# Windowed attention and a spatially gated MLP on one core: a written-out order of 1113 steps is replaced by another

## The chip, the core and the metric

The kernel runs on one core of a Trainium2 chip. The core has five engines with a queue each, which run their own instructions in order and wait for one another through semaphores: TensorE (PE), VectorE (DVE), ScalarE (ACT), GpSimd (POOL) and SyncE (SP), which here issues the transfers. The metric is the device time of one execution in microseconds, and what is compared is the median of several executions.

## What is computed

Eight batches of eight heads, 576 positions and 64 values per head go through causal attention with a window of 64. The result, 512 values per position, goes through a gated MLP whose gate is mixed over positions.

```python
# q, k, v: (8, 8, 576, 64) float32
scores = q @ k.transpose(0, 1, 3, 2) / sqrt(64)
attn = softmax(where((rel >= 0) & (rel < 64), scores, -1e9))      # rel = row - column
x = heads_side_by_side(attn @ v)                                  # (8, 576, 512)
h = maximum(x @ w_in, 0.0)                                        # w_in: (512, 1024)
u, v = h[..., :512], h[..., 512:]
v_n = (v - mean(v)) / sqrt(var(v) + 1e-6)
v_s = einsum('ts,bsd->btd', w_spatial, v_n) + b_spatial[None, :, None]
out = (u * v_s) @ w_out                                           # (8, 576, 512)
```

## The kernel before

The kernel builds a list of steps, each with a name, a function that issues its instructions and the buffers that it takes. A long string, ORDER, names all 1113 steps in the order in which they are issued; each word is `step:engine:buffer`. The engines' queues run side by side, so the string sets the order on each engine, the engine of each step that can run on several, and the buffer or PSUM bank that it gets. There is no other scheduling.

The steps of batch b (0 to 7); g is a half of four heads, u a pair of heads in it:

- `ldq`, `ldk`, `ldv`: loads, on SP (lines 424 and 445). `cq`, `ck`: casts of q and k to 16 bits; `tq`, `tk`: transposes of them on DVE (line 431). `cv`, `sl`, `su`, `s4`: v cast and copied once more, shifted by 64 positions. These casts and copies (helper `cp`, lines 316 to 324) can run on ACT or POOL, in the first two batches on DVE too. On POOL a cast of q or k is three instructions.
- `S`: scores, 56 small matmuls into a pair of banks (line 491); `E`: exp on ACT (498); `M`: the mask, as a minimum, on DVE (501); `Z`: sums of the exps by matmul (514); `N`, `n`: ln and exp on ACT, which give the inverse (541, 543); `P`: the product with v (526); `X`: the product of both on DVE (534). The last 64 positions of all heads have steps of their own, with `r` in their names.
- `V`: the gate half of x times w_in (four row blocks, and `V_4` for the last 64 rows, which also computes the last rows of the output of the batch before); `Vr`: relu on ACT (660); `Vb`, `Va`: mean and variance on DVE (662, 664); `L1`, `L2`: the inverse root on ACT (707, 709); `A`: the normalization on DVE (719).
- `U`: the other half, `Ur`: its relu on ACT (748); `G`: the mixing over positions; `Ge`: the gating on DVE (778); `O`: the product with w_out; `Oe`: its copy out of PSUM on ACT (637); `st`: stores, on SP.

A G needs all five A of its batch, an O the Ge of rows 0 to 3, a V all four X; every PE step also needs the bank that it writes to be emptied by the step that reads it. The four single banks and two pairs of banks are handed out in ORDER. Casts of the weights are `cwin`, `cwsp`, `cwo`, `cb`; `W` transposes w_spatial and `We` copies it out. `D` are 27 matmuls of zeros that fill PE early on.

The wide matmuls of V, U, G and O run through `halves`. A step in the set HALVED issues each matmul as two with 64 columns of weights (line 613), which keeps the array divided as Z and P have it; any other issues one with 128 (line 610). Before, the set comes from a rule on the neighbours in ORDER and holds 92 steps.

Of the kernel before, what the change touches and what calls it, by code (L numbers as in the profile page):

```python
# [24 lines left out]
M0_11:DVE ldv0_04:DQ Z0_00:PE:1 E0_r0:ACT:0 sl0_10:DVE:0 cv0_00:DVE:1 E0_r1:ACT Z0_10:PE:2
ldv0_13:DQ M0_r:DVE Z0_01:PE:3 ldv0_14:DQ N0_10:ACT:0 D10:PE:0 sl0_00:DVE:1 N0_01:ACT:1 su0_00:DVE
ldwin110:DQ:7 cv0_01:DVE N0_00:ACT:2 ldwin111:DQ su0_01:DVE sl0_01:POOL Z0_r:PE:2 su0_10:DVE
Z0_11:PE:3 ldwin101:DQ N0_r:ACT:3 D9:PE:0 s40_0:POOL tk1_0:DVE:5 n0_00:ACT ldb:DQ:1 D8:PE:1
ldk1_1:DQ:2 n0_10:ACT D13:PE:2 ldq1_1:DQ:3 n0_01:ACT P0_01:PE:0 cv0_11:DVE ldwin000:DQ:0 P0_00:PE:1
sl0_11:DVE su0_11:POOL N0_11:ACT:4 S1_0:PE:0:1 ldwin001:DQ X0_00:DVE:0 ldwin010:DQ:4 n0_11:ACT  # L30
cwin110:POOL D20:PE:2 s40_1:DVE ldwin011:DQ E1_00:ACT:1 D19:PE:3 cwin111:POOL X0_01:DVE P0_10:PE:1
ldwsp3:DQ:5 P0_11:PE:2 cwin101:POOL E1_01:ACT:0 X0_10:DVE:1 D18:PE:3 ldwsp2:DQ:7 D3:PE:0 X0_11:DVE
cwin100:ACT P0_r:PE:1 M1_00:DVE n0_r:ACT cb:ACT V0_1:PE:3 ldwsp1:DQ:6 M1_01:DVE ck1_1:POOL:2
V0_2:PE:0 X0_r:DVE:0 Vr0_1:ACT:0 ldwsp4:DQ:1 Z1_00:PE:2 Vb0_1:DVE:0 V0_0:PE:1 N1_00:ACT:5
ldv1_00:DQ:2 cq1_1:POOL:3 tk1_1:DVE:0 Vr0_2:ACT:1 V0_3:PE:3 Vr0_0:ACT:2 cwin000:ACT ldwsp0:DQ:2
n1_00:ACT Z1_01:PE:2 V0_4:PE:0 D25:PE:1 D26:PE:1 ldv1_01:DQ cwin010:POOL tq1_1:DVE:1 cwin001:ACT
N1_01:ACT:2 cwin011:POOL ldv1_02:DQ Vr0_3:ACT:3 Vb0_2:DVE:1 S1_1:PE:0:1 cwsp3:POOL ldv1_03:DQ
Vr0_4:ACT:4 Vb0_0:DVE:2 U0_2:PE:1 E1_11:ACT:2 cwsp2:POOL Vb0_3:DVE:3 U0_3:PE:2 Va0_2:DVE cwsp1:POOL
E1_10:ACT:3 Va0_3:DVE Va0_1:DVE Vb0_4:DVE:4 U0_4:PE:3 Va0_0:DVE Va0_4:DVE M1_11:DVE ldv1_04:DQ
L10:ACT:0 U0_1:PE:0 Ur0_3:ACT:0 M1_10:DVE ldk2_0:DQ:3 Ur0_2:ACT:1 S1_r:PE:1:0 ldv1_10:DQ:3 cwsp4:DVE  # L40
Z1_11:PE:2 L20:ACT Ur0_1:ACT:2 U0_0:PE:1 A0_4:DVE cwsp0:DVE E1_r0:ACT:1 ldv1_11:DQ E1_r1:ACT
A0_0:DVE:0 Ur0_4:ACT:3 W0:PE:0 A0_3:DVE:1 ldq2_0:DQ:0 N1_11:ACT:1 cv1_00:DVE:2 cv1_01:POOL W2:PE:3
ldv1_12:DQ M1_r:DVE Ur0_0:ACT:4 W3:PE:2 ldv1_13:DQ sl1_00:ACT:2 sl1_01:POOL W4:PE:1 We0:DVE
s41_0:ACT We2:DVE We3:ACT W1:PE:0 su1_01:POOL su1_00:DVE Z1_r:PE:3 We4:ACT ldv1_14:DQ ck2_0:POOL:0
A0_2:DVE:2 P1_01:PE:2 N1_r:ACT:0 P1_00:PE:1 ldk2_1:DQ:4 Z1_10:PE:3 A0_1:DVE:3 ldwo10:DQ:5 We1:DVE
N1_10:ACT:4 ldq2_1:DQ:7 X1_00:DVE:2 G0_4:PE:0 n1_01:ACT ldwo00:DQ:6 G0_3:PE:3 n1_10:ACT ldwo11:DQ
cv1_10:POOL:3 X1_01:DVE ldwo01:DQ tk2_0:DVE:2 sl1_10:ACT:3 su1_10:POOL G0_0:PE:1 cq2_0:ACT:1
ldq3_0:DQ:1 cv1_11:POOL ldv2_00:DQ:0 Ge0_3:DVE:0 s41_1:POOL G0_2:PE:2 sl1_11:ACT Ge0_4:DVE:1
su1_11:POOL n1_r:ACT tq2_0:DVE:3 n1_11:ACT ldk3_0:DQ:2 G0_1:PE:3 ck2_1:POOL:2 cwo10:ACT ldv2_01:DQ
Ge0_2:DVE:2 P1_10:PE:0 P1_11:PE:2 X1_10:DVE:3 S2_0:PE:1:0 X1_11:DVE cq2_1:POOL:3 ldv2_02:DQ  # L50
P1_r:PE:0 E2_00:ACT:0 Ge0_0:DVE:3 U1_2:PE:2 ldv2_03:DQ Ge0_1:DVE:4 E2_01:ACT:1 U1_1:PE:1 X1_r:DVE:1
M2_00:DVE Ur1_2:ACT:5 V1_3:PE:3 cwo01:POOL tk2_1:DVE:0 cwo11:ACT Ur1_1:ACT:0 cwo00:POOL V1_1:PE:0
Vr1_3:ACT:5 M2_01:DVE cq3_0:POOL:0 V1_2:PE:2 Vr1_1:ACT:6 ldv2_10:DQ:1 Vb1_3:DVE:5 V1_4:PE:1
ldv2_11:DQ tq2_1:DVE:1 Vr1_2:ACT:7 Z2_01:PE:3 Vr1_4:ACT:4 V1_0:PE:0 ck3_0:POOL:1 Vb1_2:DVE:1
N2_01:ACT:3 tq3_0:DVE:4 S2_1:PE:1:0 Oe0_4:ACT:0 ldv2_12:DQ Vr1_0:ACT:2 U1_0:PE:2 ldk3_1:DQ:3
cv2_00:POOL:1 Va1_2:DVE E2_11:ACT:3 Va1_3:DVE ldv2_13:DQ Vb1_1:DVE:3 Z2_00:PE:3 O0_2:PE:1 ldv2_14:DQ
Vb1_0:DVE:0 E2_10:ACT:2 Vb1_4:DVE:2 ldv2_04:DQ U1_4:PE:0 N2_00:ACT:5 Va1_1:DVE ldv3_10:DQ:2
S2_r:PE:0:1 Va1_0:DVE Va1_4:DVE tk3_0:DVE:5 L11:ACT:1 O0_0:PE:3 Oe0_2:ACT:0 ldq3_1:DQ:0 E2_r0:ACT:0
ldv3_11:DQ Ur1_4:ACT:3 M2_11:DVE U1_3:PE:1 L21:ACT ldv3_12:DQ E2_r1:ACT A1_4:DVE Oe0_0:ACT:1
O0_1:PE:0 A1_2:DVE:4 ldq4_0:DQ:4 Ur1_0:ACT:1 A1_3:DVE:5 ldv3_13:DQ A1_1:DVE:6 Ur1_3:ACT:4  # L60
S3_0:PE:0:1 A1_0:DVE:7 ldv5_10:DQ:3 n2_00:ACT M2_10:DVE Z2_11:PE:3 Oe0_1:ACT G1_0:PE:2 M2_r:DVE
sl2_00:ACT:0 su2_00:POOL Z2_r:PE:1 N2_11:ACT:2 G1_3:PE:0 Ge1_0:DVE:5 s42_0:ACT cv2_10:POOL:0
N2_r:ACT:4 ldv3_00:DQ:0 n2_01:ACT Z2_10:PE:3 Ge1_3:DVE:6 P2_00:PE:2 ldq4_1:DQ:7 N2_10:ACT:1
O0_3:PE:1 ldk4_0:DQ:5 X2_00:DVE:0 sl2_10:ACT:1 su2_10:POOL P2_01:PE:0 G1_4:PE:3 s42_1:ACT X2_01:DVE
n2_10:ACT ck3_1:POOL:2 P2_10:PE:2 Ge1_4:DVE:7 n2_11:ACT P2_11:PE:0 X2_10:DVE:1 G1_1:PE:3 E3_01:ACT:0
X2_11:DVE cq3_1:POOL:3 n2_r:ACT V2_3:PE:2 Ge1_1:DVE:8 E3_00:ACT:1 M3_01:DVE V2_2:PE:0 Oe0_3:ACT
M3_00:DVE U2_2:PE:3 st0_1:DQ Vr2_2:ACT:3 tk3_1:DVE:0 ldv4_00:DQ:1 Vr2_3:ACT:1 U2_0:PE:1 cq4_0:POOL:0
ldv3_01:DQ Ur2_2:ACT:2 tq3_1:DVE:1 Z3_00:PE:0 ldv3_02:DQ V2_0:PE:2 N3_00:ACT:0 ldv3_03:DQ
cq4_1:POOL:1 Vb2_3:DVE:4 Ur2_0:ACT:1 S3_1:PE:1:0 n3_00:ACT tq4_0:DVE:2 P2_r:PE:3 U2_3:PE:0
E3_11:ACT:2 cv3_10:POOL:2 ldv3_14:DQ X2_r:DVE:0 E3_10:ACT:3 V2_1:PE:1 Vb2_2:DVE:1 st0_4:DQ  # L70
tq4_1:DVE:3 ck4_0:POOL:2 ldk4_1:DQ:6 U2_4:PE:3 Vr2_0:ACT:0 st0_0:DQ S3_r:PE:0:1 Vr2_1:ACT:4
V2_4:PE:2 ldv3_04:DQ M3_10:DVE Ur2_4:ACT:4 Ur2_3:ACT:3 sl3_10:POOL:2 Z3_01:PE:1 E3_r0:ACT:1
# [796 lines left out]
```

## Time and profile before

| | |
|---|---|
| median of three runs | 199.47 us (199.40 to 200.56) |
| the profiled execution | 199.64 us, of which the span of instructions is 197.9 us |
| clock granted to TensorE, mean | 0.996 |
| moved by DMA | 42.71 MB, 216 GB/s over the span |

A profile page lists the busy time of each engine and its share of the span, then the span in 40 slices of 4.95 us, one digit for each: the busy tenths. PEld is the loading of weights, which overlaps the matmuls. A row of a group gives line, engine, operation, output and input tiles, shapes and count, then the time that the group keeps the engine busy, the mean of one in ns, and the idle time before them with what ended it. A row of the timeline gives start and length in us, engine, line, operation, tiles, shapes and count; in square brackets is idle time before it. The chain of waits follows the last instruction back, at each step to what released it: start, length, what.

### The profile page before, as it was taken

What the parts mean: (1) busy time and instruction counts of PE and PEld (TensorE: products, weight loads), DVE (VectorE), ACT (ScalarE), POOL (GpSimd) and SP (SyncE); (2) the same over time, 40 slices, a digit from 0 to 9 for tenths busy, and PEclk for the clock granted to TensorE, in tenths of its full rate; (3) what the DMA queues carried; (4) which work ended last, traced back from release to release, by engine and by line L of the source; (5) the groups of instructions that cost most, each with busy time, mean ns of one, the idle gap of its engine ahead of it and who ended that gap; (6) DMA issues with size and microseconds to landing.
All of it is one profiled execution on the core that took longest, in us unless ns stands there. A gap on an engine that the chain in (4) does not pass through costs nothing.

```text
span 197.9 us, 7455 instructions
## 1 busy us (share of the span) xinstructions
PE 186.3 (94%) x3145; PEld 108.1 (55%) x3145; DVE 158.2 (80%) x306; ACT 169.0 (85%) x305; POOL 77.8 (39%) x147
## 2 busy tenths in 40 slices
PE   7688999997999999999999999999999999999991
PEld 2333556664556755575476566466465565754450
...
ACT  2589889887899999999999999999999999558341
POOL 5232863964858797212999199100000000000000
...
GB/s 224 389 289 200 392 358 249 292 374 360 133 235 313 274 213 280 314 196 285 282 259 250 278 261 49 251 202 229 238 107 65 47 45 2 215 0 3 181 110 187
DMA packets 50276, 42.71 MB, mean 216 GB/s; under 512 B 39361, under 2 KB 39489, under 8 KB 50242
## 3 DMA queue, kind: packets, MB, share of 16 engines
...
## 4 chain that ended last, share of the span: by engine, by line
ACT 40%; PE 27%; DVE 17%; DMA 6%; SPq 4%; issue 4%; ACTq 0%; DVEq 0%
PE bank L613 14%; PE bank L610 8%; ACT e L498 7%; ACT ob L637 5%; ACT ru L748 5%; ACT lz L541 5%; ACT hs L316 4%; ACT lz L543 4%; SPq L445 4%; DMA nv<-in_v_dram 3%; ACT vs L660 3%; DMA nk<-in_k_dram 2%; DVE kT L431 2%; DVE e L501 2%; DVE qT L431 2%
## 5 line engine op out<-in xcount | busy, mean ns | idle before, releaser
L498 ACT ACTIVATE e<-pair 128x1024 f16<-128x1024 f32 x32 | 31.9, 1025 | 2.8 <-PE pair L491 2.6
L613 PE MATMUL bank<-wspT,vn 128*64 128x512 f16 (+3 forms) x440 | 32.4, 296 | 0.3
L778 DVE TENSOR_TENSOR g<-bank,ru 128x512 f16<-128x512 f32 (+1 forms) x40 | 24.6, 630 | 9.4 <-PE bank L610 4.4
L662 DVE BATCH_NORM_STATS2 st<-vs 128x6 f32<-128x512 f16 (+1 forms) x40 | 26.0, 672 | 3.5 <-ACT vs L660 3.4
L660 ACT ACTIVATE vs<-bank 128x512 f16<-128x512 f32 (+1 forms) x40 | 23.3, 601 | 5.7 <-PE bank L613 3.9
L534 DVE TENSOR_TENSOR x<-bank,lz 128x512 f16<-128x512 f32 x32 | 21.4, 683 | 5.7 <-PE bank L526 3.9
L748 ACT ACTIVATE ru<-bank 128x512 f32<-128x512 f32 (+1 forms) x40 | 21.7, 564 | 5.0 <-PE bank L610 4.4
L637 ACT COPY ob<-bank 128x512 f32<-128x512 f32 (+1 forms) x39 | 22.9, 592 | 2.1 <-PE bank L610 1.9
L613 PEld LDWEIGHTS <-vn 128*64 128x64 f16 (+1 forms) x440 | 18.7, 110 | 10.8 <-issue 1.2
L501 DVE TENSOR_TENSOR e<-e,mask 128x1024 f16<-128x1024 f16 x32 | 22.1, 706 | 1.2 <-ACT e L498 1.2
L319 POOL CAST hk<-nk 128x384 f16<-128x384 f32 x33 | 16.4, 531 | 16.1 <-DMA nk<-in_k_dram 15.3
L613 PE MATMUL bank<-x,win 128*64 128x512 f16 (+1 forms) x288 | 22.3, 298 | 0.0
L613 PE MATMUL bank<-win,x 128*64 128x512 f16 x184 | 22.1, 379 | 0.2 <-DVE x L603 0.2
L431 DVE STREAM_TRANSPOSE qT<-hq 128x576 f32<-128x576 f32 x16 | 19.8, 1238 | 2.3 <-POOL hq L319 2.3
L431 DVE STREAM_TRANSPOSE kT<-hk 128x576 f32<-128x576 f32 x16 | 19.9, 1244 | 0.2 <-ACT hk L316 0.2
L543 ACT ACTIVATE lz<-lz 128x512 f32<-128x512 f32 x32 | 19.8, 637 | 0.1
L541 ACT ACTIVATE lz<-bank 128x512 f32<-128x512 f32 x32 | 18.6, 607 | 1.2 <-PE bank L514 1.0
L719 DVE TENSOR_SCALAR vn<-vs,mv,ln 128x512 f16<-128x512 f16 (+1 forms) x40 | 15.6, 442 | 4.8 <-ACT ln L709 4.7
L319 POOL CAST hq<-nq 128x384 f16<-128x384 f32 x30 | 15.3, 545 | 8.3 <-DMA nq<-in_q_dram 5.7
L322 POOL COPY hs<-hv 64x512 f16<-64x512 f16 (+1 forms) x28 | 15.6, 588 | 5.0 <-issue 4.3
L818 PE MATMUL bank<-scratch 128*128 128x512 f16 (+1 forms) x68 | 15.1, 372 | 1.3 <-DVE scratch L257 1.3
L613 PE MATMUL bank<-wout,g 128*64 128x512 f16 x128 | 16.1, 380 | 0.0
...
## 6 DMA issues: line engine op xcount, KB each, us to landing
nq<-in_q_dram SPq DMA_DIRECT2D x16, 576.0 KB, 6.3
nk<-in_k_dram SPq DMA_DIRECT2D x16, 576.0 KB, 5.7
...
```

The lines of the kernel that those rows point to most:

```text
L319: nc.gpsimd.tensor_copy(o[:, n:n + 384], i[:, n:n + 384])
L431: d = add(f"t{name}{b}_{g}", ("DVE", 1.09), key, lambda e: nc.vector.transpose(qt.t[:, :].rearrange("p (i j) -> p j i", j=18), h.t[:, :].b ...
L498: ex = add(f"E{b}_{g}{u}", ("ACT", 0.91), key, lambda e, u=u: nc.scalar.activation(e2[u].t[:, :, :], sc[u].t[:, :, :], AF.Exp, bias=0.0, s ...
L501: mins.append(add(f"M{b}_{g}{u}", ("DVE", 0.65), key, lambda e, u=u: nc.vector.tensor_tensor(e2[u].t[:, :, :], e2[u].t[:, :, :], mask[:, : ...
L541: a = add(f"N{tag}", ("ACT", 0.06 + 0.00083 * n), key, lambda e: nc.scalar.activation(lz.t[:, 0:n], zb.t[:, 0:n], AF.Ln), deps=[z], acq=[l ...
L543: c = add(f"n{tag}", ("ACT", 0.09 + 0.00083 * n), key, lambda e: nc.scalar.activation(lz.t[:, 0:n], lz.t[:, 0:n], AF.Exp, bias=0.0, scale= ...
L613: nc.tensor.matmul(o[c:c + 64, :], w[:, c:c + 64], x, start=start, stop=stop)
L637: lambda e: (nc.vector.tensor_copy if last else nc.scalar.copy)(view(), m.t[rows, 0:n]),
L660: rl = add(f"Vr{b}_{j}", ("ACT", 0.49), key, lambda e: nc.scalar.activation(vs.t[0:jn, :], m.t[0:jn, :], AF.Relu), deps=[pv], acq=[vs], us ...
L662: s1 = add(f"Vb{b}_{j}", ("DVE", 0.6), key + 0.02, lambda e: nc.vector.bn_stats(st6.t[0:jn, 0:6], vs.t[0:jn, :]), deps=[rl], acq=[st6], us ...
L748: lambda e, m=m, ru=ru, n=n: nc.scalar.activation(ru.t[:, 0:n], m.t[:, 0:n], AF.Relu), deps=[pu], acq=[ru], uses=[m])))
L778: lambda e, m=m, g=g, ru=ru, n=n: nc.vector.tensor_tensor(g.t[:, 0:n], m.t[:, 0:n], ru.t[:, 0:n], ALU.mult),
```

## The change

ORDER is replaced. The steps are the same, and so is the order of the 155 DMA issues of SP. New are the order of the steps on PE, ACT, DVE and POOL, the buffers and banks, the engine of 55 casts and copies, and the set of halved steps, which is now written into ORDER (engine `PH`) and holds 118: 36 that were whole are halved, 10 that were halved are whole.

```diff
 ORDER = """
-ldq0_0:DQ:0 ldk0_0:DQ:1 D14:PE:0 ldk0_1:DQ:2 ldq0_1:DQ:3 D12:PE:1 ldv0_00:DQ:0 D23:PE:2 ldq1_0:DQ:4
...
+D0:PE:0 D21:PE:1 D4:PE:2 D13:PE:3 ldq0_0:DQ:0 ldk0_0:DQ:1 D14:PE:0 D1:PE:1 cq0_0:POOL:0 tq0_0:DVE:0
...
+su1_11:POOL n1_11:ACT sl1_11:POOL P1_10:PE:2 X1_00:DVE:2 cq2_1:POOL:2 cwo00:POOL ldv2_14:DQ
...
+P1_11:PE:0 X1_11:DVE G0_0:PH:1 Ge0_0:DVE:2 ck2_1:ACT:3 ldq3_1:DQ:5 ldv3_11:DQ V1_3:PH:2 tk2_1:DVE:0
+tq2_1:DVE:1 Vr1_3:ACT:5 Vb1_3:DVE:5 sl2_00:POOL:0 V1_0:PH:0 cwo10:ACT cq3_0:POOL:1 Ge0_2:DVE:3
+Vr1_0:ACT:6 Vb1_0:DVE:1 V1_1:PH:1 Vr1_1:ACT:7 ldv3_12:DQ su2_00:POOL E2_00:ACT:1 ldq4_0:DQ:0
+ldv3_13:DQ U1_0:PH:2 V1_2:PH:0 P1_r:PE:1 Vr1_2:ACT:4 Vb1_2:DVE:2 cv2_10:POOL:0 S2_1:PE:0:1
+s42_0:POOL n1_r:ACT X1_r:DVE:1 Va1_2:DVE cwo01:DVE Ur1_0:ACT:5 E2_10:ACT:3 M2_10:DVE M2_01:DVE
+sl2_10:POOL:1 U1_2:PH:3 E2_11:ACT:2 Ur1_2:ACT:1 G0_3:PH:0 V1_4:PE:2 Oe0_4:ACT:0 Vb1_1:DVE:3
+Vr1_4:ACT:1 Va1_1:DVE s42_1:POOL cq3_1:POOL:3 U1_4:PH:1 Ur1_4:ACT:4 M2_00:DVE S2_r:PE:0:1
+E2_r0:ACT:0 E2_r1:ACT U1_3:PH:3 Ur1_3:ACT:2 Ge0_3:DVE:4 Z2_00:PE:2 N2_00:ACT:4 Va1_0:DVE O0_2:PH:1
...
-G7_0:PE:0 U7_1:PE:1 Ge7_0:DVE:5 Ge7_3:DVE:6 G7_1:PE:3 Ur7_1:ACT:1 U7_4:PE:0 Ge7_1:DVE:7 G7_4:PE:2
-Ur7_4:ACT:5 O7_2:PE:1 Ge7_4:DVE:9 O7_0:PE:3 Oe7_2:ACT:1 st7_2:DQ O7_1:PE:0 Oe7_0:ACT:0 st7_0:DQ
...
+Ur7_1:ACT:1 G7_1:PE:1 Ge7_1:DVE:6 Ge7_0:DVE:5 G7_3:PE:3 Ge7_3:DVE:7 G7_2:PE:2 G7_4:PE:1 Ge7_2:DVE:8
+O7_2:PE:0 Oe7_2:ACT:0 O7_0:PE:3 O7_1:PE:2 O7_3:PE:0 st6_1:DQ Oe7_0:ACT:1 st7_2:DQ st7_0:DQ
+Ge7_4:DVE:9 Oe7_1:ACT st7_1:DQ O7_4:PE:1 Oe7_3:ACT Oe7_4:DVE:0 st7_3:ACT st7_41:ACT st7_40:DQ
 """
...
-        out.append((by.pop(name), eng, [int(x) for x in banks]))
+        out.append((by.pop(name), "PE" if eng == "PH" else eng, [int(x) for x in banks]))
...
-def halved(longest):
...
-HALVED = halved(2) | {f"U0_{i}" for i in range(5)}
+HALVED = {w.split(":")[0] for w in ORDER.split() if w.split(":")[1] == "PH"}
```

Which casts and copies move:

| | from ACT | to ACT |
|---|---|---|
| casts of q and k | ck0_1, ck4_1, ck7_0, ck7_1, cq5_0, cq7_0, cq7_1 to POOL | ck2_1, ck3_1, ck6_1, cq5_1 from POOL |
| v: cv, sl, su, s4 | 3 cv, 8 sl, 3 su, 7 s4 to POOL | su2_10, s41_1, s45_0 from POOL |
| weights | cb, cwin001, cwo11 to POOL; cwin100, We3 to DVE | cwin111 from POOL; We0, We2 from DVE |

Between DVE and POOL: cq0_1, three cv and a sl of batch 0, cwsp0 and cwsp4 go to POOL; sl0_01, s40_0, cq1_1, su1_01 and cwo01 come from it.

More of the change, by code (lines that the diff above doesn't have):

```diff
@@ L25 @@
[L25 to L72, printed above, removed]
@@ new lines @@
+ldv2_03:DQ su1_00:DVE ck2_0:POOL:3 Z1_10:PE:0 N1_10:ACT:3 su1_01:DVE tk2_0:DVE:2 G0_4:PE:3
+Ge0_4:DVE:0 s41_0:POOL G0_1:PE:1 Ge0_1:DVE:1 cq2_0:ACT:1 sl1_01:POOL n1_00:ACT cv1_10:POOL:3
+sl1_10:ACT:3 s41_1:ACT ldv2_10:DQ:1 Z1_11:PE:2 tq2_0:DVE:3 ldv2_11:DQ N1_11:ACT:2 ldv2_12:DQ
+ldk3_1:DQ:4 ldv2_13:DQ n1_10:ACT P1_00:PE:0 G0_2:PE:3 P1_01:PE:1 S2_0:PE:1:0 su1_10:POOL cv1_11:POOL
+su1_11:POOL n1_11:ACT sl1_11:POOL P1_10:PE:2 X1_00:DVE:2 cq2_1:POOL:2 cwo00:POOL ldv2_14:DQ
+ldv2_04:DQ cwo11:POOL ck3_0:POOL:0 X1_01:DVE E2_01:ACT:0 ldv3_10:DQ:2 X1_10:DVE:3 cv2_00:POOL:1
@@ new lines @@
+A4_3:DVE:3 cq6_1:POOL:1 ldv7_02:DQ tq6_1:DVE:1 Vr5_3:ACT:1 V5_0:PH:0 Vr5_0:ACT:6 A4_4:DVE G4_3:PH:3
+M6_00:DVE S6_1:PE:1:0 E6_10:ACT:2 Ge4_3:DVE:1 Vb5_0:DVE:0 P5_r:PE:1 X5_r:DVE:1 G4_4:PH:2 Ge4_4:DVE:0
+E6_11:ACT:1 M6_01:DVE cv6_10:POOL:0 G4_1:PH:0 V5_4:PE:3 Vb5_1:DVE:5 Vr5_4:ACT:7 Z6_00:PE:1
+N6_00:ACT:0 s46_0:POOL Oe4_4:ACT:0 G4_2:PH:2 Ge4_1:DVE:2 n6_00:ACT sl6_10:POOL:1 M6_10:DVE
+Vb5_4:DVE:1 U5_2:PH:0 Ur5_2:ACT:4 Z6_10:PE:1 G4_0:PH:3 N6_10:ACT:4 n6_10:ACT Vb5_3:DVE:3 Z6_01:PE:0
+N6_01:ACT:5 Va5_4:DVE su6_00:POOL P6_00:PE:1 M6_11:DVE Ge4_2:DVE:3 s46_1:POOL Va5_0:DVE ldv7_03:DQ
@@ new lines @@
+Va6_4:DVE N7_01:ACT:2 n7_01:ACT Va6_2:DVE G5_2:PH:3 S7_r:PE:0:1 Z7_00:PE:2 N7_00:ACT:0 n7_00:ACT
+Ge5_2:DVE:8 G5_0:PH:1 Z7_10:PE:0 N7_10:ACT:4 Va6_0:DVE U6_2:PH:3 P7_01:PE:2 Ur6_2:ACT:2 P7_00:PE:0
+Ge5_0:DVE:9 O5_1:PH:1 E7_r0:ACT:1 Vb6_3:DVE:5 Va6_3:DVE O5_0:PH:3 L16:ACT:0 X7_00:DVE:2 M7_11:DVE
+L26:ACT A6_3:DVE:0 Oe5_0:ACT:1 Oe5_1:ACT X7_01:DVE O5_2:PH:0 U6_3:PH:2 Oe5_2:ACT:0 A6_0:DVE:1
+n7_10:ACT O5_3:PH:3 sl7_10:POOL:3 su7_10:POOL A6_1:DVE:2 E7_r1:ACT st5_4:DQ U6_4:PH:1 ldv7_14:DQ
+M7_r:DVE Oe5_3:ACT A6_2:DVE:3 A6_4:DVE G6_3:PH:0 Z7_11:PE:3 Ur6_4:ACT:1 s47_1:POOL Ur6_3:ACT:0
@@ L194 @@
 CHOOSE = as_listed
-def halved(longest):
-    def kind(name):
-        return "s" if name[0] == "S" else "v" if name[0] in "ZP" or (
-            name[0] == "V" and name.endswith("_4")) else "f"
-    seq = [w.split(":")[0] for w in ORDER.split() if w.split(":")[1] == "PE" and w[0] != "D"]
-    runs = []
-    for name in seq:
-        if not runs or runs[-1][0] != kind(name):
-            runs.append((kind(name), []))
-        runs[-1][1].append(name)
-    out = set()
-    for a, (what, names), c in zip([("f", [])] + runs, runs, runs[1:] + [("f", [])]):
-        near = (a[0] == "v") + (c[0] == "v")
-        if what == "f" and not any(n[0] == "W" for n in names) and (
-                near == 2 or near == 1 and len(names) <= longest):
-            out.update(names)
-    return out
-HALVED = halved(2) | {f"U0_{i}" for i in range(5)}
+HALVED = {w.split(":")[0] for w in ORDER.split() if w.split(":")[1] == "PH"}
 @with_exitstack
```

175 lines of the change are left out of this document (98 added, 77 removed).

## The prediction

> **What bounds the kernel now.** I read the page's busy shares and slices first, then a window sum, the chain of waits, and TensorE's timeline step by step.
>
> ```profile
> span 197.9 us, 7455 instructions
> PE 186.3 (94%) x3145; PEld 108.1 (55%) x3145; DVE 158.2 (80%) x306; ACT 169.0 (85%) x305; POOL 77.8 (39%) x147
> ...
> PE   7688999997999999999999999999999999999991
> ...
> ACT  2589889887899999999999999999999999558341
> POOL 5232863964858797212999199100000000000000
> ```
>
> ```profile
> 50.00:125.00 75.00, 74.40 (x1453) 44.90 (x1450) 68.39 (x124) 72.58 (x134) 51.69 (x96) 1.00 0.88 240
> ```
>
> The window's columns are length, then busy time of PE, PEld, DVE, ACT and POOL, clock, DMA share and GB/s. From the tenth slice on (about 50 us) PE is nearly always busy and ACT is busy 72.58 of 75 us; POOL has a third of its time free, and all of it after 125 us. But PE "busy" counts overlapping matmuls, so I price PE steps by the distance from one start to the next:
>
> ```profile
> 14.85 0.30 PE L559 MATMUL pair<-qT,kT 32*128 32x64 f16 x16
> 15.08 0.84 PE L514 MATMUL bank<-e,ones 128*64 128x512 f16 x6
> ...
> 21.70 0.25 PE L526 MATMUL bank<-e,hv 128*64 128x128 f16 x2
> ...
> 22.31 1.04 PE L818 MATMUL bank<-scratch 128*128 128x512 f16 x4
> ...
> 46.87 1.90 PE L613 MATMUL bank<-x,win 128*64 128x512 f16 x16
> 48.60 2.76 PE L613 MATMUL bank<-win,x 128*64 128x512 f16 x24
> 51.19 0.38 PE L693 MATMUL bank<-win,x 128*64 128x512 f16 x1
> ...
> 52.05 0.38 PE L514 MATMUL bank<-e,ones 128*64 128x512 f16 x2
> 52.27 1.03 PE L613 MATMUL bank<-win,x 128*64 128x512 f16 x8
> 53.23 0.67 PE L491 MATMUL pair<-qT,kT 32*128 32x128 f16 x56
> 53.83 0.41 PE L613 MATMUL bank<-x,win 128*64 128x512 f16 x2
> ...
> 60.46 1.25 PE L613 MATMUL bank<-wspT,vn 128*64 128x512 f16 x10
> 61.54 0.28 PE L582 MATMUL bank<-er,ones 128*64 128x128 f16 x4
> ...
> 179.88 1.89 PE L610 MATMUL bank<-x,win 128*128 128x512 f16 x8
> 181.60 1.89 PE L610 MATMUL bank<-wout,g 128*128 128x512 f16 x8
> ...
> 188.53 0.63 PE L610 MATMUL bank<-x,win 128*128 128x64 f16 x16
> 188.99 0.76 PE L610 MATMUL bank<-wspT,vn 128*128 128x64 f16 x20
> 189.59 3.62 PE L610 MATMUL bank<-wout,g 128*128 128x512 f16 x16
> 193.14 0.63 PE L802 MATMUL bank<-wout,g 128*64 128x256 f16 x8
> ```
>
> Three halved U steps take 51.19 - 48.60 = 2.59 us, 0.863 each; two whole steps take 181.60 - 179.88 = 1.72, 0.86 each. So a V, U or O step costs 0.863, halved or whole. A G step costs 1.08 (60.46 to 61.54), V_4 0.86, Z 0.22, S 0.60, S_r 0.23, U_4 0.46, G_4 0.60. U before S takes 0.96 (52.27 to 53.23): a change of the array's division costs 0.10. Two P steps and one such change take 0.61 (21.70 to 22.31), so a P is 0.25; I estimate Z_r, half a Z, at 0.11 and P_r, 8 of a P's 14 matmuls, at 0.14.
>
> Before, from U1_2 at 46.87 to O7_4 at 193.14, the list has 28 U, 28 V and 32 O (their _4 steps not among them), 28 G, 7 V_4, 7 U_4, 7 G_4, 11 S, 6 S_r, 24 Z, 6 Z_r, 24 P, 6 P_r and 22 changes of division: 142.6 us. The trace has 193.14 - 46.87 = 146.3. So after 47 us PE loses only 3.7 us. That is the prize in the long middle; the start is a race with the loads.
>
> **The change, part by part.** (1) *Casts and copies.* 55 change engine. Their rows:
>
> ```profile
> L316 ACT COPY hs<-hv 64x768 f16<-64x768 f16 x7 | 5.8, 830 | 0.2
> L316 ACT CAST hk<-nk 128x1152 f16<-128x1152 f32 x5 | 5.8, 1156 | 4.4 <-DMA nk<-in_k_dram 4.4
> ```
>
> ```profile
> 43.65 1.40 POOL L319 CAST hk<-nk 128x384 f16<-128x384 f32 x3 [1.02 <-DMA nk<-in_k_dram]
> ```
>
> ACT gives up 7 casts of q or k (1.156 each, 8.1 us), 6 sl copies (0.83, 5.0) and 20 others, most of them smaller (at an estimated 0.65, 13); it takes on 4 such casts (4.6) and 6 smaller steps (3.7). Net 26 - 8 = 18 us off ACT. POOL pays 1.40 for a cast that costs ACT 1.156, so about 21 us go onto POOL. POOL's 77.8 become about 99 of 198: it has the room, if it isn't late at one place. DVE gives nine small steps and takes seven: its sum hardly changes.
>
> (2) *The start, to S2_1.* The order of transfers is the same and the early transfers run one behind another, so I keep their landings. The last gates are the two halves of q of batch 2:
>
> ```profile
> 33.42 0.45 SPq L424 DMA_DIRECT2D nq<-in_q_dram  x1
> ...
> 38.38 0.38 SPq L424 DMA_DIRECT2D nq<-in_q_dram  x1
> ```
>
> ```profile
> nq<-in_q_dram SPq DMA_DIRECT2D x1, 576.0 KB, 6.3
> ...
> nq<-in_q_dram SPq DMA_DIRECT2D x1, 576.0 KB, 8.8
> ```
>
> ```profile
> L431 DVE STREAM_TRANSPOSE qT<-hq 128x576 f32<-128x576 f32 x16 | 19.8, 1238 | 2.3 <-POOL hq L319 2.3
> ```
>
> The last number of a DMA line is the time from issue to landing. The second half lands at 38.38 + 8.8 = 47.2; POOL's cast (1.40) ends at 48.6, DVE's transpose (1.24) at 49.85, and S2_1 starts there. Behind that cast POOL holds two casts of w_out and k of batch 3, which are needed only from V1_4 (about 52) on. PE is ready for S2_1: S2_0 waits in the same way for the first half (33.42 + 6.3, cast by ACT in 1.16, transposed by 42.2), and the nine steps between hold 0.60 + 2 x 0.25 + 1.08 + 5 x 0.863 + 0.14 and two changes, 6.8 us, so PE arrives at about 49.0. From S2_1 the new list has 27 U, 24 V, 32 O, 29 G, 7 V_4, 7 U_4, 7 G_4, 11 S, 6 S_r, 24 Z, 6 Z_r, 24 P, 6 P_r and 18 changes: 139.0 us.
>
> The wait has a price: tq2_1 stands in DVE's in-order queue, and behind it stand eight steps of 512 or 1024 columns, X1_r, a cast of w_out, two short ones and then Ge0_3, for which O0_2 waits.
>
> ```profile
> 177.53 1.27 DVE L662 BATCH_NORM_STATS2 st<-vs 128x6 f32<-128x512 f16 x2
> ```
>
> ```profile
> L778 DVE TENSOR_TENSOR g<-bank,ru 128x512 f16<-128x512 f32 x32 | 21.4, 682 | 8.3 <-PE bank L610 3.5 <-PE bank L613 2.8 <-ACT ru L748 1.0
> ```
>
> Two batch-norm steps in 1.27 us, one of which shows 0.67, make a pace of 0.60: 8 x 0.60 + 0.35 + 0.35 + 0.15 + 0.68 = 6.3 us, so O0_2 can't start before 56.1. PE's own steps between S2_1 and O0_2 hold 5.3 us (0.60, 2 x 0.863, 1.08, 0.86, 0.46, 0.23, 0.22, a change) and would be done at 55.15. PE loses 0.9. Without any later loss O7_4 would start at 49.85 + 0.9 + 139.0 = 189.75; by the same sum before has 46.87 + 142.6 = 189.5. The start is a draw, to within 1 us: an earlier landing gives at most the 0.8 that PE waits for S2_1 and the 0.9 behind it, another miss of that size takes as much.
>
> (3) *The middle.* What becomes of before's 3.7 us of losses? Two places in the chain of waits show their kind:
>
> ```profile
> 167.48 0.48 ACT ob L637
> 168.01 0.82 PE bank L613 x40
> ```
>
> PE's G step starts the moment ACT has emptied its bank. By the bank numbers in the list most of the late losses are of this kind, and ACT, with 72.58 of 75 us busy, is what makes banks late. With some 18 us less on ACT I halve the loss: 1.9 us. Its ends are 0 and all of 3.7. About 0.25 of it is new and sure: at the end the new list has G7_2, G7_4, O7_2, and O7_2 needs Ge7_2. The last matmul of G7_2 starts 0.86 after its first and shows 0.38, Ge7_2 takes 0.68, together 1.92, against 1.08 + 0.60 = 1.68 of PE work; before, U7_4 (0.46) stood between too and hid it.
>
> (4) *Halves.* 36 steps are newly halved and 10 no longer: nothing by the 0.863 and 0.86 above, and the changes of division that they spare are in the 18 against 22.
>
> (5) *Stores* stay where they were in SP's queue, but their waits end with ACT copies that come no later; loads behind them aren't held. Nothing.
>
> Sum: 189.75 + 1.9 = 191.65, plus the same end (197.9 - 193.14 = 4.76) is a span of 196.4; with the 1.74 us around the span (199.64 - 197.9) 198.15. The profiled execution is 0.17 above the median of 199.47, so 198.0.
>
> **Rivals.** *POOL stands in DVE's way (slower).*
>
> ```profile
> 100.57 2.35 DVE L719 TENSOR_SCALAR vn<-vs,mv,ln 64x512 f16<-64x512 f16 x4
> 181.65 1.70 DVE L719 TENSOR_SCALAR vn<-vs,mv,ln 128x512 f16<-128x512 f16 x5 [1.21 <-ACT ln L709]
> ```
>
> ```profile
> 100.50 2.28 POOL L322 COPY hs<-hv 64x512 f16<-64x512 f16 x4
> ```
>
> Beside a running POOL four A steps take 2.35 us (0.59 each), alone five take 1.70 (0.34): 1.25 us per batch, right before G. Before, POOL is idle after 125 us; in the new list it works into batch 7, and A4_4 and A6_2 stand directly before their G. If the G of batches 4, 5 and 6 each wait in full, 3.75 us come on top: 201.8. It decides where POOL is running at those moments; against it, POOL has half its time free and can run ahead. The Trainium skill (SBUF — State Buffer, section "SBUF: two separate sides") says that DVE and GpSimd share a port pair as an exclusive lock, and the loser waits for the other's whole instruction. By that rule the trace's 0.59 against 0.34 is the lock; a copy of 0.61 us could hold an A longer than these rows show.
>
> *PE's losses aren't ACT's (no change).* If bank waits are only handed on to DVE, busy 68.39 of 75 us, the 3.7 stays: 189.75 + 3.7 + 4.76 + 1.74 - 0.17 = 199.8.
>
> *All slack is used (faster).* Late losses of 0.5 and the wait for S2_1 half gone: 198.0 - 1.4 - 0.8 = 195.8.
>
> **Numbers.** Forecast 0.40 (196.9 to 199.0), no change 0.18 (199.0 to 200.5), faster 0.20 (195 to 196.9), POOL's rival 0.22 (200.5 to 204). 1%, 2.0 us, is about what a measurement can tell here. Faster by over 1% is below 197.5: 0.20 and 0.15 of the forecast, 0.35. Slower is above 201.5: 0.17 of the rival. The rest, 0.48, is within. The range that leaves out 2 in 10 is 195.9 to 202.3.
>
> **What would show it.** ACT's busy time near 151 and POOL's near 99; S2_1 at 49.8 and O0_2 at 56; O7_4 at 191.7; PE's distance from S2_1 to O7_4 at 141.8. If A steps of batches 4 to 6 show 0.6 with POOL beside them and G right behind, the rival holds. If q2_1 lands elsewhere than 47.2, part (2) is wrong; if PE still loses over 3 us after 56, part (3) is.

## The result, and the profile after

The changed kernel takes 201.89 us (median of four runs, 200.53 to 203.43), the kernel before, measured beside it, 199.44. The ratio is 1.0114, with a 95% interval of 1.0073 to 1.0155: it is slower, by a little over 1%, where 198.0 and slightly faster was forecast. The profiled execution took 202.22 us at a granted clock of 1.000. (Below, executions more than 1.5% longer than the fastest of the same kernel are left out of every ratio; a_pool_memset and b_pool_short have only profiles of such executions, at clocks of 0.661 and 0.758, and of these nothing is read but rows and busy time of VectorE and GpSimd.)

First the page of the changed kernel: span, busy time, and the slices of the engines that the forecast named.

```profile
span 200.5 us, 7771 instructions
PE 187.3 (93%) x3289; PEld 110.4 (55%) x3289; DVE 162.5 (81%) x304; ACT 154.6 (77%) x282; POOL 105.8 (53%) x189
...
ACT  2379788679999889979887799888977987437521
POOL 5563748685399877821999898707429300000000
```

ACT gave up 14.4 us (169.0 to 154.6), as the change meant it to. POOL took 28.0 (77.8 to 105.8), and in the slices it now works up to the 32nd, where it was idle from the 27th on. But DVE, whose list of work hardly changed, is 4.3 us busier than before (158.2). The groups tell where. Two of them, first of the changed kernel, then of the kernel before (count, busy us, mean ns of one, idle time before):

```profile
L481 DVE TENSOR_TENSOR e<-e,mask 128x1024 f16<-128x1024 f16 x32 | 24.6, 779 | 1.3 <-ACT e L478 1.2
...
L699 DVE TENSOR_SCALAR vn<-vs,mv,ln 128x512 f16<-128x512 f16 (+1 forms) x40 | 17.8, 493 | 2.2 <-ACT ln L689 2.2
```

```profile
L501 DVE TENSOR_TENSOR e<-e,mask 128x1024 f16<-128x1024 f16 x32 | 22.1, 706 | 1.2 <-ACT e L498 1.2
...
L719 DVE TENSOR_SCALAR vn<-vs,mv,ln 128x512 f16<-128x512 f16 (+1 forms) x40 | 15.6, 442 | 4.8 <-ACT ln L709 4.7
```

The same 32 masks (M) take 2.5 us more and the same 40 scalings (A) 2.2 us more. What stands beside them is seen in the timeline of the changed kernel (start, length, engine, what, count), DVE first, then POOL in the same stretch:

```profile
113.73 2.76 DVE L481 TENSOR_TENSOR e<-e,mask 128x1024 f16<-128x1024 f16 x3
```

```profile
113.17 0.51 POOL L299 CAST hk<-nk 128x384 f16<-128x384 f32 x1
113.62 2.32 POOL L299 CAST hq<-nq 128x384 f16<-128x384 f32 x3
115.89 1.07 POOL L302 CAST hv<-nv 128x512 f16<-128x512 f32 x1
```

Three masks take 0.92 each, and POOL's casts beside them 0.77 each where one alone takes 0.51: each engine holds the other up. Matched instruction by instruction, 7 masks with next to nothing on POOL have a mean of 682 ns, and 22 with POOL beside them nearly throughout 806; for scalings it is 401 (21 of them) and 639 (15). In the changed kernel POOL runs for half or more of the time of 24 of the 32 masks; before, of 8.

What it costs is read at the instruction behind it. The G step G3_4 of the changed kernel, where the five scalings of batch 3 stand before it (DVE, POOL, PE; in square brackets idle time and what ended it):

```profile
102.19 2.79 DVE L699 TENSOR_SCALAR vn<-vs,mv,ln 128x512 f16<-128x512 f16 x5
```

```profile
101.45 1.48 POOL L299 CAST hk<-nk 128x384 f16<-128x384 f32 x3
102.87 1.28 POOL L302 CAST hv<-nv 128x512 f16<-128x512 f32 x2
104.22 1.01 POOL L302 COPY hs<-hv 64x512 f16<-64x512 f16 x2
```

```profile
103.32 1.05 PE L593 MATMUL bank<-wout,g 128*64 128x512 f16 x8
105.03 0.82 PE L593 MATMUL bank<-wspT,vn 128*64 128x64 f16 x40 [0.65 <-DVE vn L699]
```

The length of these five is not new: their single durations add up to 3.10 us here and to 3.18 in the kernel before, where G followed them with a wait of 0.10. New in length are those of batches 1 and 2 (3.11 and 2.87, before 1.99 and 2.02). All waits of PE behind S2_1 that the profile lists in the changed kernel, who waits and for whom, in us in total, how often and the longest, are these:

```profile
PE bank L593 <- DVE vn L699: 0.7, 1, 0.7
PE pair L471 <- issue: 0.6, 1, 0.6
PE bank L593 <- issue: 0.4, 1, 0.4
PE bank L593 <- DVE g L758: 0.4, 1, 0.4
PE bank L593 <- DVE x L514: 0.4, 1, 0.4
```

"issue" is time in which PE waited for nothing that the profile shows. Each wait that names an engine names DVE. Counted down to 0.03 us, PE's idle times behind S2_1 are 2.6 us here, and in the kernel before 0.8 after 47 us. These are lower bounds, since matmuls overlap and a short wait leaves no gap between two of them.

Last, the two marks that the forecast set on PE, S2_1 and O7_4:

```profile
51.59 0.67 PE L471 MATMUL pair<-qT,kT 32*128 32x128 f16 x56
...
196.03 0.63 PE L782 MATMUL bank<-wout,g 128*64 128x256 f16 x8
```

From the one to the other are 144.44 us, of which 139.0 are the work as the prediction priced it: PE loses 5.4. By the same sum before lost 3.7. So against the forecast's span of 196.4 the ledger is: 1.74 from S2_1 (51.59 instead of 49.85), 2.64 between the marks (144.44 instead of 141.8), 0.29 gained behind O7_4 (4.47 instead of 4.76). That is 4.1, and 196.4 + 4.1 = 200.5.

### The profile page after: what moved, and what is told of

Its sections match the earlier page's. It is cut to its first block, busy times and chain, and to the rows that moved or that the text cites. A ratio compares the mean times of both kernels' runs of the same rounds, so it can differ in the third digit from the quotient of the medians.

```text
span 200.5 us, 7771 instructions
## 1 busy us (share of the span) xinstructions
PE 187.3 (93%) x3289; PEld 110.4 (55%) x3289; DVE 162.5 (81%) x304; ACT 154.6 (77%) x282; POOL 105.8 (53%) x189
## 4 chain that ended last, share of the span: by engine, by line
PE 55%; DVE 15%; DMA 12%; SPq 8%; ACT 5%; issue 3%; POOL 0%; ACTq 0%; POOLq 0%
PE bank L593 39%; PE bank L590 6%; SPq L425 6%; DMA wi<-in_moe_w_in_dram 4%; DVE e L481 4%; DMA ws<-in_moe_w_spatial_dram 3%; DMA nq<-in_q_dram 3%; DVE st L642 3%; PE bank L506 3%; DVE vn L699 2%; PE pair L471 2%; PE bank L494 2%; DMA nv<-in_v_dram 2%; SPq L404 2%; DVE g L758 1%
## 5 line engine op out<-in xcount | busy, mean ns | idle before, releaser
L593 PE MATMUL bank<-wspT,vn 128*64 128x64 f16 (+3 forms) x480 | 34.6, 288 | 1.1 <-DVE vn L699 0.7
L593 PE MATMUL bank<-x,win 128*64 128x512 f16 (+1 forms) x400 | 30.6, 292 | 0.4 <-DVE g L758 0.4
L593 PE MATMUL bank<-win,x 128*64 128x512 f16 x240 | 30.0, 380 | 0.4 <-issue 0.4
L299 POOL CAST hk<-nk 128x384 f16<-128x384 f32 x36 | 20.5, 606 | 18.0 <-DMA nk<-in_k_dram 17.6
L299 POOL CAST hq<-nq 128x384 f16<-128x384 f32 x36 | 19.4, 574 | 17.2 <-DMA nq<-in_q_dram 9.6
L302 POOL COPY hs<-hv 64x512 f16<-64x512 f16 (+1 forms) x44 | 25.4, 604 | 1.0
L481 DVE TENSOR_TENSOR e<-e,mask 128x1024 f16<-128x1024 f16 x32 | 24.6, 779 | 1.3 <-ACT e L478 1.2
L593 PE MATMUL bank<-wout,g 128*64 128x512 f16 x208 | 25.5, 380 | 0.0
L593 PEld LDWEIGHTS <-win 128*64 128x64 f16 x400 | 15.9, 111 | 8.8 <-issue 0.3
L593 PEld LDWEIGHTS <-x 128*64 128x64 f16 x240 | 14.4, 110 | 10.5 <-DVE er L553 0.9
```

The lines of the kernel that those rows point to most:

```text
L299: nc.gpsimd.tensor_copy(o[:, n:n + 384], i[:, n:n + 384])
L302: nc.gpsimd.tensor_copy(o[:, lo:hi, :, :], i[:, lo:hi, :, :])
L481: mins.append(add(f"M{b}_{g}{u}", ("DVE", 0.65), key, lambda e, u=u: nc.vector.tensor_tensor(e2[u].t[:, :, :], e2[u].t[:, :, :], mask[:, : ...
L593: nc.tensor.matmul(o[c:c + 64, :], w[:, c:c + 64], x, start=start, stop=stop)
```

## The experiments

The theory behind them: GpSimd, loaded with 28 us more, stands beside VectorE's masks and scalings and makes them longer, VectorE comes late to PE, and that eats what the new order gains. The rivals: the new order itself is worse; GpSimd is merely late with its own casts; the halves cost something; the slow start is all of it. Step names are those of the order: M masks, A scalings, cq, ck, cv, sl, su casts and copies.

**The two kernels again** (a_again, b_again), unchanged, to see what of a trace is luck.

> The changed kernel, unchanged. Its first trace has the last w_spatial at 35.3 us and the first half of q of batch 2 at 42.1, over 2 us behind the first trace of before, and S2_1 at 51.6. Theory 'the new list delays the loads': the same landings again, 35 and 42, while before lands at 33 and 40 on the same chip. Rival 'luck of the run': both kernels land within 0.5 us of each other here. The second loss, 5.4 us of TensorE from S2_1 to the last step against 3.7 before, should come again within 1 us either way.

> The kernel before, unchanged, for a second trace from the chip on which the others of this group run. In the first trace the last part of w_spatial landed at 33.1 us and the first half of q of batch 2 at 39.7. If the early loads vary from run to run or from chip to chip, some of these landings move by over 1 us here; if they are fixed by the list, they come within 0.3 us of those.

The changed kernel took 201.97 us, ratio 1.0109 (1.0068 to 1.015); the kernel before 200.2 in its one execution. Masks 773 and 731 ns, losses of PE after 47 us 5.0 and 4.2: the late losses and the long masks repeat, though the distance between the kernels in them is smaller than in the first pair. The start does not: S2_1 of the changed kernel comes at 50.6 instead of 51.6. The issue of the first half of q of batch 2 on SP's queue shows why. Before, changed, and the repeat of the changed one:

```profile
33.42 0.45 SPq L424 DMA_DIRECT2D nq<-in_q_dram  x1
```

```profile
35.66 0.45 SPq L404 DMA_DIRECT2D nq<-in_q_dram  x1
```

```profile
34.58 0.45 SPq L404 DMA_DIRECT2D nq<-in_q_dram  x1
```

In the repeat of the kernel before it is issued at 35.31. So the loads come 1 to 2 us earlier or later from one execution to the next, in both kernels.

**Order or engines** (a_old_engines, b_new_engines). The 55 changes of engine, without the rest, and the rest without them:

```diff
 # a_old_engines: the new order, these on the engines they had
-sl2_00:POOL:0
+sl2_00:ACT:0
...
 # b_new_engines: the order of before, these on the new engines
-sl2_00:ACT:0
+sl2_00:POOL:0
...
```

> The new list, but the 55 casts and copies on the engines that they had before. Theory 'GpSimd beside VectorE': minimum steps (M) beside GpSimd fall from 24 to about 10, their mean from 779 ns to 705 and that of A from 493 to 445; VectorE's busy time falls from 162.5 to about 158 and TensorE's loss after S2_1 from 5.4 us to 3.5: about 200 us. Rival 'the order itself': the loss stays at 5 us or more, and with some 18 us more on ScalarE the time is 202 or above.

> The list of before, but the 55 casts and copies on the engines of the change. Theory 'GpSimd beside VectorE': VectorE's busy time rises by 3 to 5 us, the means of M and A to about 780 and 490 ns, and the time to 201 or more. Rival 'ScalarE was the limit': the time falls below 199.0.

The old order with the new engines takes 201.84 us, ratio 1.0106 (1.0063 to 1.0149): the changes of engine alone give a slowdown of the whole change's size, though not in the same places. The masks are long there too (803 ns), but some 2 us are lost by S2_1 already (55.2, against 53.2 and 53.3 in the two profiles of the kernel before), and from S2_1 to O7_4 it takes 140.8 us, hardly more than before (139.9 and 140.4): long masks cost little where PE does not wait for them. Why the start is late there, no run tells. The new order with the old engines takes 231.55 (1.1611, 1.1569 to 1.1652), and from S2_1, which comes at 62.0, to O7_4 PE loses 23.7 us at a granted clock of 0.963. By the letter that is what the rival expected (202 or above), and this run alone does not refute it; the next experiment does, where the new order on its own engines, with most of GpSimd's data left out, is faster than the kernel before. What the run shows is that an order and its engines belong together, and undoing a move is not the opposite of making it. A later experiment shows such a place.

**GpSimd taken out of the way** (a_pool_short, b_pool_short). From batch 2 on its casts and copies of q, k and v move an eighth of their columns. The instructions and their order stay; buffers of these tiles are made once and kept, so the columns that are not written hold old values.

```diff
-nc.gpsimd.tensor_copy(o[:, n:n + 384], i[:, n:n + 384])
+nc.gpsimd.tensor_copy(o[:, n:n + w], i[:, n:n + w])      # w = 48 from batch 2 on
...
-nc.gpsimd.tensor_copy(o[:, lo:hi, :, :], i[:, lo:hi, :, :])
+nc.gpsimd.tensor_copy(o[:, lo:hi, :, 0:w], i[:, lo:hi, :, 0:w])      # w = 8
```

> The changed kernel; from batch 2 on GpSimd's casts and copies of q, k and v move only an eighth of their columns (the rest of these buffers keeps old values, so the output is not the reference's). Lists, engines and instruction counts stay. Theory 'GpSimd beside VectorE': the mean of M falls from 776 to about 700 ns, that of A from 492 to about 430, VectorE's busy time from 162.5 to about 159; TensorE's loss after S2_1 from 5 to about 2.5 us, the time to about 199. Rival 'the new order itself': the losses at Z3_00 (0.8 to 1.3 us) and G3_4 (0.9) stay and the time stays above 201.

> The same shortening in the kernel before (its output is not the reference's either). It has less GpSimd work to shorten. Theory 'GpSimd beside VectorE': M and A fall too, to about 690 and 420 ns, but little of it was on TensorE's path: 198.5 to 199.4. Rival 'GpSimd lateness, not the neighbourhood, matters': before gains as much as the changed kernel does.

The changed kernel then takes 197.55 us, ratio to the kernel before 0.9898 (0.9853 to 0.9943): faster than before, and near the forecast's 198.0, though by another sum: S2_1 comes 1.5 us later than forecast, and PE loses 1.2 us less behind it (1.6, where 0.9 and 1.9 were forecast). The page and the groups of it:

```profile
PE 185.8 (95%) x3289; PEld 110.2 (56%) x3289; DVE 158.6 (81%) x304; ACT 153.9 (78%) x282; POOL 59.0 (30%) x189
```

```profile
L494 DVE TENSOR_TENSOR e<-e,mask 128x1024 f16<-128x1024 f16 x32 | 22.6, 717 | 0.7 <-ACT e L491 0.7
...
L712 DVE TENSOR_SCALAR vn<-vs,mv,ln 128x512 f16<-128x512 f16 (+1 forms) x40 | 14.4, 409 | 1.9 <-ACT ln L702 1.9
```

and the same place before G3_4 (DVE, then PE, where no wait is left):

```profile
100.20 1.76 DVE L712 TENSOR_SCALAR vn<-vs,mv,ln 128x512 f16<-128x512 f16 x5
```

```profile
101.38 1.05 PE L606 MATMUL bank<-wout,g 128*64 128x512 f16 x8
102.26 0.80 PE L606 MATMUL bank<-wspT,vn 128*64 128x64 f16 x40
```

Masks are back at 717 ns, the five scalings at 1.76 us, and PE's late losses fall from 5.4 to 1.6, though S2_1 (51.3) starts as late as it did. Of PE's waits the profile lists none any more, and its idle times behind S2_1, 2.6 us in the changed kernel, are 0.2. In the kernel before the same edit gives 0.998 (0.9952 to 1.0009), nothing that can be measured. So the gain is not that less data is moved as such: it is there only where GpSimd had been put in the way. What it does not tell is whether GpSimd disturbs VectorE, or is itself late with its casts, since it is shorter in both respects.

**Busy, but not reading** (a_pool_memset). GpSimd does one narrow copy for each step and fills the full width with zeros.

```diff
-nc.gpsimd.tensor_copy(o[:, n:n + 384], i[:, n:n + 384])
+nc.gpsimd.memset(o[:, n:n + 384], 0.0)      # after a copy of o[:, 0:48]
```

> The changed kernel; from batch 2 on, GpSimd's casts and copies of q, k and v each do one narrow copy (48 columns, or 8 of 64) and then fill their whole width with zeros, so GpSimd writes as much as before, reads almost nothing, and its output is not the reference's. Theory 1 (VectorE slows down where GpSimd reads the on-chip memory beside it): masks back to about 700 ns (from 773 to 779), scalings of A to about 420 ns, the loss of TensorE after 47 us falls from 5 to 2.5, 198.5 us. Theory 2 (it is enough that GpSimd writes beside it): masks 740 ns or more, 200.5 to 201.5 us. Theory 3 (VectorE isn't slowed to any effect; GpSimd itself brings its casts too late, so the time goes with GpSimd's busy time): busy time above 95 us and 201 to 202 us.

199.05 us, ratio 0.9967 (0.9925 to 1.0009). GpSimd is busy for 100.2 us, and most of the loss is gone all the same: its lateness is not the cause. The rows show how finely the two effects part. A mask beside fills, DVE then POOL:

```profile
114.96 0.68 DVE L502 TENSOR_TENSOR e<-e,mask 128x1024 f16<-128x1024 f16 x1
```

```profile
114.70 1.14 POOL L313 MEMSET hqk<- 128x384 f16 x3
```

and five scalings beside fills:

```profile
69.30 2.24 DVE L720 TENSOR_SCALAR vn<-vs,mv,ln 128x512 f16<-128x512 f16 x5 [1.11 <-ACT ln L710]
```

```profile
69.85 1.55 POOL L313 MEMSET hqk<- 128x384 f16 x3
```

The mask takes what it takes alone (four masks with fills for most of their time have a mean of 683 ns). The scalings are still held up: 2.24 against 1.76 (eight of them with fills for most of their time: 576 to 1059 ns, mean 695). Theory 1 holds for the masks; for the scalings it is enough that GpSimd writes, as theory 2 has it. With the masks freed and the scalings not, the kernel gets back 1.5% of the time, against 2.2% in a_pool_short; the two intervals overlap, so how PE's loss divides between masks and scalings is not settled.

**Longer and shorter pieces** (a_pool_whole, a_pool_fine). The full data again, in one instruction for each step or in about twice as many.

```diff
-for n in (0, 384, 768):
-    nc.gpsimd.tensor_copy(o[:, n:n + 384], i[:, n:n + 384])
+nc.gpsimd.tensor_copy(o, i)                  # a_pool_whole
...
+for n in range(0, 1152, 192):                # a_pool_fine
+    nc.gpsimd.tensor_copy(o[:, n:n + 192], i[:, n:n + 192])
```

> The changed kernel with GpSimd's casts in one instruction of 1152 columns instead of three of 384, and its copies in one instead of two. If VectorE only loses while both want the memory at the same moment, in proportion to the overlap: masks stay within 30 ns of 779, and the time within 1% of 201.9 us. If an instruction of GpSimd holds VectorE's instruction for as long as it lasts: masks about 900 ns in the mean, and 204 us or more. If GpSimd's own lateness is the cause: the three fixed costs become one, GpSimd's busy time falls below 100 us and the time to about 200.5 us.

> The changed kernel with GpSimd's casts in six instructions of 192 columns instead of three of 384, and its copies in one for each block of 64 columns times four. If an instruction of GpSimd holds VectorE's instruction for as long as it lasts, shorter ones let go sooner: masks about 720 ns, 200 us. If the loss goes by overlap alone: masks 770 to 800 ns, GpSimd's busy time 5 to 10 us higher by the additional fixed costs, and the time 202 to 203 us.

Whole: 204.77 us, 1.0241 (1.0174 to 1.0309), with GpSimd busy 14 us less (91.4). Fewer fixed costs, and slower: again not lateness. The masks' mean is 817 ns, less than the 900 expected, because fewer of them meet GpSimd (17 of 32); those that meet it pay more. One such mask, DVE then POOL:

```profile
99.50 1.63 DVE L479 TENSOR_TENSOR e<-e,mask 128x1024 f16<-128x1024 f16 x1
```

```profile
99.28 1.31 POOL L298 CAST hk<-nk 128x1152 f16<-128x1152 f32 x1
```

The cast ends at 100.59, the mask 0.54 later: it waited for the whole cast, and did most of its work after it. Fine: 202.65 us, 1.0132 (1.0064 to 1.0199), and masks of 807 ns, where 720 was expected if short pieces let go sooner. Most do: without the two longest (1.78 and 1.46 us) the mean is 752. Those two are let in late. The longest:

```profile
119.61 1.78 DVE L481 TENSOR_TENSOR e<-e,mask 128x1024 f16<-128x1024 f16 x1
```

```profile
119.42 1.44 POOL L302 CAST hv<-nv 128x256 f16<-128x256 f32 x4
```

The piece that was running when this mask came and the three behind it go by before the mask gets its turn, and PE waits 2.27 us for it. The scalings gain: their mean falls from 493 ns to 433, and the five of batch 1, which took 2.80 us in the changed kernel, take turns with GpSimd's pieces:

```profile
60.06 1.77 DVE L699 TENSOR_SCALAR vn<-vs,mv,ln 128x512 f16<-128x512 f16 x5
```

```profile
59.93 2.11 POOL L299 CAST hq<-nq 128x192 f16<-128x192 f32 x6
```

But GpSimd is busy for 124.0 us, 18 more than with longer pieces, where 5 to 10 were expected. So these shorter pieces relieve the scalings, but not the masks and not the kernel.

**The halves** (a_rule_halves): the rule of before, applied to the new order.

```diff
-U0_3:PE:0
+U0_3:PH:0
...
-G1_2:PH:2
+G1_2:PE:2
...
```

> The changed kernel with another set of gMLP steps in halves: those that the rule of the kernel before takes in the new order (111 instead of 118; 102 are in both sets). The forecast's part on halves (a halved step costs TensorE what a whole one does): the same within 0.3%, 201.3 to 202.5 us. The rival (the set of halves matters, by the changes of the array's division or by their effect on the clock or the evictions): another time by more than 0.5%.

Ratio 1.0141 (1.0092 to 1.0191), against 1.0114 and 1.0109 for the changed kernel: no gain and no loss that these intervals could tell from each other. That is weaker than the 0.3% expected: its ten executions spread from 201.25 to 208.02, with a median of 204.0 over all of them, so a loss of half a per cent or more could hide in it.

**Which moves** (b_moves_start, b_moves_mid, b_moves_67: the order of before with 25, 15 or 15 of the 55; a_undo_start, a_undo_mid, a_undo_67: the new order with the same ones undone). Each diff is of the form shown for the 55, for the steps of batches 0 and 1 and the weights, of batches 2 to 5, or of batches 6 and 7.

> The list of before; of the 55 moves only the 25 of batches 0 and 1 and of the weights. With all 55 the list of before took 201.84 and reached S2_1 1.9 us later than without. Theory 'the start': all of that 2.4 us is here, 201.5 or more. Theory 'GpSimd beside VectorE later': 199.5 to 200.5.

> The list of before; of the 55 moves only the 15 of batches 2 to 5. Theory 'GpSimd beside VectorE': M beside GpSimd rises, TensorE's loss after 60 us goes from 4 to about 5 us: 200 to 200.8. Theory 'the start': no change, 199.0 to 199.7. Relief of ScalarE, as the forecast had it: 198 to 199.

> The kernel before with only the 15 moves of batches 6 and 7, where its GpSimd is idle after 125 us. Forecast's part on ScalarE (its late losses of 3.7 us come from ScalarE emptying banks late): losses after 60 us fall by 1 to 2 us, 197.5 to 198.5 us. Theory (no mask that matters lies there): masks 706 to 735 ns as before, and between 199 and 200 us, the same. Rival (GpSimd beside the scalings of batches 5 to 7 slows them): 200.5 us or more.

In the old order: 1.0109 (1.0028 to 1.0191), 1.0047 (1.0006 to 1.0087) and 0.999 (0.9966 to 1.0014). By the ratios the moves of the start cost the most there (S2_1 at 55.0, nearly as late as with all 55), though the intervals of the first two overlap; those of the end cost nothing that can be measured. b_moves_mid took the 200.1 us that the theory gave it, but not by its sign: its masks stay at 707 ns, 9 of 32 beside GpSimd, and the one long wait of PE in its profile (1.66 us, in the slowest of its ten executions) is for an exp on ACT, behind a cast that waited for q. So it says nothing for the theory. The last one is a point against the forecast by itself:

```profile
PE 186.9 (95%) x3145; PEld 107.7 (55%) x3145; DVE 161.0 (81%) x306; ACT 158.7 (80%) x292; POOL 92.9 (47%) x172
```

ACT is relieved of 10.3 us (169.0 to 158.7) in the part where POOL had nothing to do, and PE's losses after 60 us are 3.9, as in the kernel before (3.4 and 4.0). Its masks, at 760 ns, are longer than the theory expected of it, and the time is no longer for it; that a gain from ACT and a loss from the masks cancel, no run rules out.

> The changed kernel with the 25 moves of batches 0 and 1 and of the weights undone; the other 30 stay. Backlog theory (what the start puts on GpSimd is still queued there in batches 2 to 4): masks beside GpSimd 14 or fewer of 32, mean below 745 ns, and 199.5 us or less unless the start itself now waits. Rival (the new list is fitted to its engines, and any part of the moves undone makes it wait in the start, as all 55 undone did: 231.55 us): S2_1 later than 53 us (51.59 in the changed kernel) and more than 204 us.

> The changed kernel with the 15 moves of batches 2 to 5 undone. If these moves put GpSimd beside the masks: masks below 745 ns and 200 us or less. If the backlog of the start does: masks stay above 760 ns and the time within 0.7% of 201.9 us. Rival (fitted list): single waits of TensorE of over 2 us after 60 us, and more than 204 us.

> The changed kernel with the 15 moves of batches 6 and 7 undone, so that ScalarE has 11 steps of batch 7 more. Their masks and scalings come after the stretch that loses the time, so by the theory nothing is gained: masks within 25 ns of 779, 201.5 to 202.5 us. If ScalarE is late with them (the forecast's part on ScalarE): TensorE waits for bank emptying after 130 us, more than 203 us.

In the new order all three are much slower: 211.37 (1.0601, 1.0548 to 1.0654), 220.85 (1.1103, 1.1037 to 1.117) and 216.38 (1.0839, 1.0796 to 1.0883). So the question which moves put GpSimd beside the masks could not be answered by undoing them; the rival, an order fitted to its engines, is what they show (of a_undo_67 neither expectation came true as it was put: its masks fell to 743 ns, and its largest wait, 4.51 us, stands at 112 us before P4_00). The backlog theory falls besides: without the start's moves still 24 of 32 masks stand beside GpSimd, mean 807 ns. In a_undo_mid one sees how it goes wrong (POOL, DVE, PE):

```profile
53.04 1.42 POOL L288 CAST hk<-nk 128x384 f16<-128x384 f32 x3 [3.08 <-DMA nk<-in_k_dram]
54.40 1.18 POOL L291 CAST hv<-nv 128x512 f16<-128x512 f32 x2
55.52 1.42 POOL L288 CAST hk<-nk 128x384 f16<-128x384 f32 x3
```

```profile
56.97 1.26 DVE L400 STREAM_TRANSPOSE kT<-hk 128x576 f32<-128x576 f32 x1 [8.77 <-POOL hk L288]
```

```profile
57.63 1.92 PE L582 MATMUL bank<-win,x 128*64 128x512 f16 x8 [6.70 <-ACT vs L629]
```

ck2_1, back on POOL, stands there behind ck3_0, which waits for k of batch 3 and runs at 53.04. So ck2_1 ends at 56.9, DVE has waited 8.77 us for it, and PE stops for 6.70: ACT, for which PE waits, had been standing at sl2_00, which needs cv2_00, the step of POOL between the two.

No kernel that computes everything came out faster than the kernel before beyond its interval.

## Why the prediction was wrong

(1) *Casts and copies.* The sizes were right for ACT (151 forecast, 154.6) and somewhat low for POOL (99, 105.8). The sentence that failed is "DVE: its sum hardly changes". Its list doesn't, its time does: 158.2 to 162.5, by 2.5 on masks and 2.2 on scalings. Part of POOL's excess is the other side of the same thing, casts of 0.51 that show 0.77 beside a mask.

(2) *The start.* S2_1 came 1.74 late (51.59), 0.7 in the repeat. Not by the mechanism given: q of batch 2's second half landed at 47.3, as forecast, but PE arrived late, since S2_0 had come at 44.7 instead of 42.2. The first half was issued at 35.66, where the prediction had kept 33.42 from the one execution before it. That landing moves by 1 to 2 us between executions of both kernels, so it was a draw with more play than the "1 us" allowed. The 0.9 behind it, O0_2 waiting for Ge0_3, measured 0.4 (from S2_1 to O0_2, at 57.28, 5.69 us against 5.28 of work) and 0.6 in the repeat, where the wait that the profile lists, 0.36, is for a mask in front of Z2_00: tq2_1 was through at 50.6, a us ahead of S2_1, so it held up nothing behind it. With 139.0 of work behind it the new order would end, without late losses, at 190.6 (51.59 + 139.0) and 189.6 in the repeat, before at 189.5.

(3) *The middle.* This is the step that decides: 3.7 us of losses were to be halved to 1.9, with 0.9 more at O0_2, and 5.4 came (5.0 in the repeat). With GpSimd out of the way 1.6 are left. So the new order does hold the gain that the step gave it, and more than all of it is given back where VectorE, its masks and scalings held up by GpSimd, comes late to PE. The reason given, ACT emptying banks late, is not borne out: 10 us less on ACT in the last batches bring nothing that can be measured (b_moves_67), and in the profile of the kernel before PE's idle times after 47 us that end with an output copy of ACT add up to 0.15 us of 0.8. Most of the 3.7 is thus no idle time that the profile shows, but matmuls further apart than the priced distances; where it lies stays open. What of the gain is ACT's relief in the middle and what the order itself, no run tells apart.

(4) *Halves*: nothing was forecast, and nothing shows that these runs could see. (5) *Stores*: nothing forecast, nothing found late there.

*The rivals.* "POOL stands in DVE's way" was given 0.22 and 201.8 us. Its mechanism is what happened, its place is not: it named the scalings of batches 4 to 6, which in the changed kernel take 1.96, 2.26 and 2.03 us for five (single durations added), nearly the 1.94 to 2.02 that they take with GpSimd out of the way. The long ones are those of batches 1 to 3 (3.11, 2.87, 3.10; 1.92 to 2.07 without), and the masks, which the rival left out, carry the somewhat larger part of VectorE's additional time (2.5 of 4.7 us). So that its 201.8 meets the measured time is luck. The argument held against it, that POOL has half its time free and can run ahead, was the mistake: of the 27.0 us of POOL's waits that the profile lists from 50 to 150 us, 19.6 end with the landing of a load, and the loads keep it working in the same stretch in which VectorE masks and scales.
